# Two gate/up weight groups move from SP's DMA queue to ACT's, and score visits keep their order

## The chip, the cores and the metric

The kernel runs on one core of a Trainium2 chip. The metric is the device time of one execution in microseconds, lower is better. The core has a matrix engine (PE, with its weight loads as PEld), a vector engine (DVE), a scalar engine (ACT), GpSimd (POOL) and a queue engine (SP), which run their own instruction streams and wait for each other on semaphores. Transfers are done by 16 DMA engines; SP and ACT can both issue them.

## The reference, cut to what matters

```
x = A_x                                  # 1 x 2048 x 576, bf16
xn = layernorm(x)
q, k, v = split(xn @ wqkv)               # 32 heads of 18 columns
p = softmax(mask(q k^T / sqrt(18)))      # causal, a window of 256 positions
s = (p v) @ wo
h = sigmoid(xn @ w_gate) * (xn @ w_up)   # 2048 x 4608
g = silu(h @ w_down)
out = x + s * g
```

## The kernel before

The 2048 rows are worked in four chunks of 512 (`CH`, `NCH`), each of four blocks of 128 rows. A chunk goes through layer norm, the q, k and v projections, attention in 8 groups of four heads, the output projection (`wo`), the gate/up projection in 36 feature tiles of 128 (`build_ffn`), the down projection and the final product. The weights of gate and up come in 12 groups of three feature tiles into a ring of three slots (`RW`). `load9` brings one group (named `w:chunk:group`) with four DMAs of 240 or 192 KB, 884,736 bytes together.

The program first builds a list of operations with dependencies (`deps`, which become semaphore waits), order dependencies (`odeps`, which only tell the planner what comes first), an engine, a planned cost and a priority. `schedule()` then plans each engine's order with these costs, and `emit()` writes the engines' streams in that order. So a changed cost factor (`W_FACTOR` for weight loads, `XT_BYTES` for transposes) or a changed dependency can move work on all engines. DMA cost in the planner is one pipe in order of issue. In the kernel before every DMA is issued by SP.

What stands around the change, in the first chunk:

- `project` (L448) makes q, k or v of one block. q and k are copied (q by DVE at L490, k by ACT at L491) into `pk`, a ring of three slots (`RPK`), and a DMA transpose (L205, `qkt:chunk:block:q or k`) moves them into `qkp`, from which the scores read. The order of the projections is q0 q1 v0 v1 q2 v2 k0 v3 k1 q3 k2 k3 in the list (`QKV_FIRST`); a later one that takes the same `pk` slot waits for the transpose of the earlier one. k0 takes the slot of q0, k1 that of q1, q3 that of q2, k2 that of k0. v is copied by ACT (L513).
- `build_ffn` makes feature tile `ft` in steps `fa:c:ft`, `fb0:c:ft` and `fb1:c:ft` (L748), 18 matmuls per tile. The first step of a group's first tile (`fa:0:3` for the second group) waits for the group's four DMAs. ACT makes the tanh (L734), DVE the product (L738).
- `build_unit` makes one score visit (L556, `sc:c:heads:unit`; `pvsc` where it is merged with the value product of an earlier group, L639) into PSUM banks 0 to 3. ACT takes the exponentials (L579, two per visit), DVE the masks. The visits are filler between the gate/up steps, and the planner may take them in any order that their dependencies allow.
- The gate/up groups of the later chunks wait for a slot of the ring and for `w_gate`, a step of the down projection (L821).

Two places of the kernel before in its own words: after the second group's loads, the transposes from the third on are planned behind them,

```python
                    if c == 0 and fg == 1:
                        for o in self.op_qkt[QKT_BEHIND:]:
                            o.behind = ws[-1:]
```

and the banks that the down projection of a chunk's last block may take are

```python
            cands = ((0, 1), (2, 3)) if blocks[-1] == QPC - 1 else ((6, 7), (4, 5), (0, 1), (2, 3))
```

Of the kernel before, what the change touches and what calls it, by code (L numbers as in the profile page):

```python
# [15 lines left out]
QPC = CH // P  # L16
# [18 lines left out]
RW = 3  # L35
# [20 lines left out]
FB_CUTS = (0, 3, 7)  # L56
LAST = 448
W_GATE = 2

PRIO_NS = 40.0  # L60
SEM_NS = 50.0
DMA_SLACK_NS = 600.0
# [5 lines left out]
W_ISSUE_NS = 660.0  # L68
# [2 lines left out]
LATE_SLACK = 5000.0  # L71
LN_STEP = 1
XT_CUT = 4
QKT_BEHIND = 2
WARM = 10
X0_SLACK = 0.0
X_PRIO = (-9, -9, -9, -9)
QKV_LOAD = (-8, -4, -6)
W_PRIO = (-5, 2, 3)
WARM_NS = 427.0  # L80
W_FACTOR = 1.42
X0_FACTOR = 1.7
XT_BYTES = 1.2
DMA_LAT_NS = 1600.0
DMA_BYTES_PER_NS = 320.0

# [79 lines left out]
class Builder:  # L166
# [32 lines left out]
        return o  # L199

    def dma(self, dst, src, nbytes, name, lane, deps=(), prio=3, issue=DMA_ISSUE_NS, transpose=False,
            slack=DMA_SLACK_NS, eng="SP"):
        def fn(eng):
            if transpose:
                return eng.dma_start_transpose(dst, src)  # L205
            return eng.dma_start(dst, src)  # L206
        o = self.op(eng, issue, fn, name, deps, prio, nbytes=nbytes, lane=lane)
        o.slack = slack
        if lane not in self.lane_ids:
            self.lane_ids[lane] = len(self.lane_ids)  # L210
        return o
# [51 lines left out]
    def build(self):  # L263
        self.r_xr = Ring(NXR)
        self.r_xnr = Ring(NXNR)
        self.r_xn = Ring(1)
        self.r_w = Ring(RW)
        self.r_t = Ring(RT)
        self.r_pk = Ring(RPK)
        self.r_exp = Ring(NEXP)  # L270
        self.r_s = Ring(RS)
        self.r_xf = Ring(RXF)
        self.r_th = Ring(RTH)
        self.r_rec = Ring(RREC)
        self.r_bn = Ring(RBN)
        self.op_f1 = {}
        self.build_init()
        self.op_pv = [[None] * NHG for _ in range(NCH)]
        self.op_sc = [[[] for _ in range(NHG)] for _ in range(NCH)]
        self.op_on = [[None] * NHG for _ in range(NCH)]  # L280
        self.op_oc = [[[], []] for _ in range(NCH)]
        self.op_v = [None] * NQB
        self.op_tail = [None] * NHG
        self.op_hT = {}
        self.f2_last = None
        for c in range(NCH):
            self.build_ln(c)
            if c == 0:
                self.build_weights()
                self.build_wd()  # L290
            self.build_qkv(c)
            self.last_mul = None
            self.pending = None
            self.build_attn(c)
            if c == 0:
                self.op_wo = []
            self.build_wo(c)
            self.build_ffn(c)
            if c == 0:
                self.build_late_weights()  # L300
                for o in self.ops:
                    if o.name.startswith("wo:0:") and o.fence is None:
                        o.add_dep(self.op_wo)
# [27 lines left out]
            return r  # L331
        self.op_warm = self.pe(n * WARM_NS, f, name, deps=deps, prio=-9, psum=[ps])

    def load9(self, low, up, w_low, w_up, name, lane, deps, prio, factor=1.42):
        cols = w_low.shape[1]
        a = w_low.rearrange("(j p) c -> p j c", p=64)
        b = w_up.rearrange("(j p) c -> p j c", p=64)
        out = []
        for k, (dst, src, n) in enumerate(((low[:, 0:5, :], a[:, 0:NC:2, :], 5), (up[:, 0:4, :], b[:, 1:NC:2, :], 4),
                                           (low[:, 5:NC, :], a[:, 1:NC:2, :], 4), (up[:, 4:NC, :], b[:, 0:NC:2, :], 5))):  # L340
            out.append(self.dma(dst, src, factor * n * 64 * cols * 2, f"{name}.{k}", lane + (k,), deps=deps, prio=prio,
                                issue=W_ISSUE_NS))
        return out

    def build_weights(self):
# [137 lines left out]
    def build_qk(self, c, i, j, old):  # L483
        spk, dpk = self.r_pk.take()
        o, ps = self.project(c, i, j, f"qk:{c}:{i}:{j}", dpk, self.op_pv[c - 1][NHG - 1] if c > 0 else None)

        def f_ev(e):
            dst = self.pk[:, spk, :, 0:DH].rearrange("p (t h) d -> p t h d", t=2)
            if j == 0:
                return e.tensor_copy(dst, self.halves(ps))  # L490
            return e.activation(dst, self.halves(ps), ACTF.Copy)  # L491
        ev = self.rd("ACT" if j else "DVE", act_ns(D) if j else dve_ns(D), f_ev, f"qke:{c}:{i}:{j}",
                     deps=[o, self.op_pkz] + [t for t in (self.op_on[c - 1] if c > 0 else [])], prio=1, psum=[ps])
        c0 = j * CH + i * P
        dm = self.dma(self.qkp[:, :, c0:c0 + P], self.pk[:, spk, :, :].rearrange("p h d -> p (h d)"),
                      XT_BYTES * 8 * P * P * 2, f"qkt:{c}:{i}:{j}", ("qk", i, j), deps=[ev] + old, prio=0,
                      issue=XT_ISSUE_NS, transpose=True)
        self.r_pk.release(spk, dm)
        (self.op_q, self.op_k)[j].append(dm)
        self.op_qkt.append(dm)  # L500
        return o
# [40 lines left out]
    def build_unit(self, c, u, pieces, merge):  # L542
# [22 lines left out]
        if pend:  # L565
            self.pending = None
            o = self.pe(pend[1] + MODE_NS + nblk * P / 2.4 + 30, lambda e, a=pend[0], b=f_sc: (a(e), b(e))[1],
                        f"pvsc:{c}:{hgs[0]}:{u}", deps=pend[2] + deps, prio=0, psum=[pend[3], ps], mode=("c32", "r32"))
            pend[4](o)
        else:  # L570
            o = self.pe(nblk * P / 2.4 + 30, f_sc, f"sc:{c}:{hgs[0]}:{u}", deps=deps, prio=1, psum=[ps], mode="r32")
        for hg in hgs:
            self.op_sc[c][hg].append(o)
        exps = []
# [150 lines left out]
    def build_ffn(self, c):  # L725
# [25 lines left out]
        for ft in range(NFT + 1):  # L751
            if ft < NFT:
                if ft % FG == 0:
                    fg = ft // FG
                    sw, dw = self.r_w.take()
                    slots.append(sw)
                    wp = W_PRIO[fg] if c == 0 and fg < RW else -2
                    fc = slice(fg * FG * P, (fg + 1) * FG * P)
                    ws = self.load9(self.wgs[0:64, sw, :, :], self.wgs[64:P, sw, :, :], self.wg[:, fc],
                                    self.wu[:, fc], f"w:{c}:{fg}", ("w", sw),  # L760
                                    dw + ([self.w_gate] if c > 0 and fg < RW else []), wp)
                    dmas.append(ws)
                    if c == 0 and fg == 1:
                        for o in self.op_qkt[QKT_BEHIND:]:
                            o.behind = ws[-1:]
                pg.append(Psum((6,), (7,), (5,), (4,)))
                pu.append(Psum((6,), (7,), (5,), (4,)))
            war = [self.f2_last[ft // WDG]] if self.f2_last and ft < NFT else []

            def f_a(e, ft=ft):  # L770
                for i in range(NA):
                    if ft < NFT:
                        r = step(e, 0, ft, i)
                    if ft > 0:
                        r = step(e, 1, ft - 1, NC - NA + i)
                return r
            oa = self.pe(NA * mm_ns(CH), f_a, f"fa:{c}:{ft}",
                         deps=(dmas[ft // FG] + self.all_xn + war if ft < NFT else []), prio=3,
                         psum=[pg[ft]] if ft < NFT else [], mode="r64", odeps=mms)
            if ft > 0:  # L780
                pu[ft - 1].users.append(oa)
                if ft % FG == 0:
                    self.r_w.release(slots[ft // FG - 1], oa)
                th_mul(ft - 1, ob, oa)
            if ft == NFT:
                break

            def f_b(e, ft, i0, i1):
                for i in range(i0, i1):
                    step(e, 0, ft, NA + i)  # L790
                    r = step(e, 1, ft, i)
                return r
            ob = oa
            for n, (i0, i1) in enumerate(zip(FB_CUTS, FB_CUTS[1:])):
                ob = self.pe((i1 - i0) * mm_ns(CH), lambda e, ft=ft, i0=i0, i1=i1: f_b(e, ft, i0, i1), f"fb{n}:{c}:{ft}",
                             deps=[ob], prio=3, psum=[pu[ft]] if n == 0 else [], mode="r64")
                if n > 0:
                    pu[ft].users.append(ob)
            pg[ft].users.append(ob)
            self.op_f1[(c, ft)] = ob  # L800
            mms = [ob]
# [3 lines left out]
        self.f2_ops = f2_ops = {}  # L805
        prev = mms
        for blocks in (((0, 1), (2,), (3,)) if c == 0 else ((0,), (1,), (2,), (3,))):
            cands = ((0, 1), (2, 3)) if blocks[-1] == QPC - 1 else ((6, 7), (4, 5), (0, 1), (2, 3))
            banks = {i: Psum(*cands) for i in blocks}
            if c == NCH - 1 and blocks == (QPC - 1,):  # L810
                self.build_last(c, prev)
# [318 lines left out]
```

## Time and profile before

| what | value |
|---|---|
| median of 3 runs | 576.91 us (576.68 to 577.46) |
| profiled execution | 576.29 us |
| its span, first to last instruction | 574.5 us |
| mean granted PE clock | 0.998 |
| PE / ACT / DVE / POOL busy | 566.0 / 300.8 / 294.1 / 23.0 us |
| gate/up matmuls (L748) | 2592, 298.7 us busy |
| down projection matmuls (L821) | 1080, 135.0 us busy |
| q, k, v projection matmuls (L448) | 864, 55.3 us busy |
| score matmuls (L556) | 704, 36.1 us busy |
| bytes moved by DMA | 72.82 MB, mean 127 GB/s |

Matmuls overlap, so busy times of groups are sums of overlapped intervals. A wait of PE is idle time ahead of one of its instructions; the profile names what ended it where a semaphore event shows it, and writes "issue" where it shows none. The time of a DMA instruction on a queue is the time that its issue takes; "to landing" counts from the issue to the semaphore event of the data.

### The profile page before, as it was taken

The numbers are of one execution on the slowest core, as the hardware profiler recorded it, in microseconds if no ns is written. First come the engines' busy times: TensorE is split into PE (matmuls) and PEld (weight loads), VectorE is DVE, ScalarE is ACT, GpSimd is POOL, SyncE is SP. The second block draws the span as 40 slices with busy tenths as digits, with TensorE's granted clock in tenths as the row PEclk, the third lists the DMA queues.
The fourth block names the chain that finished last, engine by engine and source line by source line (L and its number), as shares of the span: only waits on it lengthen the run. The fifth ranks groups of instructions, "written<-read, shape, count | busy, mean of one in ns | idle before, by whom it ended". The sixth has DMA issues, their size and how long they took to land.

```text
span 574.5 us, 14808 instructions
## 1 busy us (share of the span) xinstructions
PE 566.0 (99%) x6350; PEld 274.7 (48%) x6350; DVE 294.1 (51%) x589; ACT 300.8 (52%) x403; POOL 23.0 (4%) x51
## 2 busy tenths in 40 slices
PE   8999999999999999999999999999999999999996
PEld 5544443457444444455753444344654444444554
DVE  5138877422247886621115888772122677774112
ACT  5357787214448887520307787760242778872201
POOL 3001110000001100000000011000000000000000
PEclk9999999999999999999999999999999999999999
DMA  8999999436935665341793666414479356651010
GB/s 203 200 214 251 224 211 232 88 63 119 198 80 135 146 156 126 79 87 42 140 206 91 146 138 151 106 50 100 56 135 186 84 124 138 134 126 40 1 42 21
DMA packets 124861, 72.82 MB, mean 127 GB/s; under 512 B 53630, under 2 KB 124286, under 8 KB 124798
## 3 DMA queue, kind: packets, MB, share of 16 engines
q1 hardware_dynamic: 124798, 71.90, 58.6%
q8 instruction: 50, 0.82, 0.6%
q14 instruction: 13, 0.11, 0.1%
HBM read 55.22 MB, written 2.36 MB: 100 GB/s over the span
## 4 chain that ended last, share of the span: by engine, by line
PE 95%; SPq 3%; DMA 1%; issue 0%; DVE 0%; ACT 0%
PE ps L748 50%; PE ps L821 23%; PE ps L448 8%; PE ps L556 5%; PE ps L639 4%; PE ps L705 3%; SPq L206 2%; PE ps L851 2%; DMA wgs<-in_B_w_up_dram 1%; SPq L205 1%; DVE thf L884 0%; ACT thf L882 0%; DVE thf L886 0%; DVE xf L888 0%
## 5 line engine op out<-in xcount | busy, mean ns | idle before, releaser
L748 PE MATMUL ps<-xn,wgs 64*128 64x512 bf16 x2592 | 298.7, 377 | 1.2 <-DMA wgs<-in_B_w_up_dram 1.2
L579 ACT ACTIVATE expr<-ps 128x1024 bf16<-128x1024 f32 (+1 forms) x184 | 174.9, 1003 | 45.3 <-PE ps L556 45.3
L748 PEld LDWEIGHTS ps<-xn,wgs 64*128 64x128 bf16 x2592 | 119.5, 94 | 152.3 <-issue 19.1
L821 PE MATMUL ps<-wd_sb,hT 128*128 128x512 bf16 (+1 forms) x1080 | 135.0, 287 | 0.0
L734 ACT ACTIVATE tring<-ps 128x512 bf16<-128x512 f32 x144 | 86.4, 600 | 62.6 <-PE ps L748 61.2
L611 DVE TENSOR_TENSOR expr<-expr,m 128x1024 bf16<-128x1024 bf16 (+1 forms) x152 | 81.9, 571 | 68.6 <-ACT expr L579 68.5
L738 DVE SCALAR_TENSOR_TENSOR hT<-tring,ps 128x512 bf16<-128x512 bf16 x144 | 97.0, 675 | 39.0 <-ACT tring L734 27.7
L821 PEld LDWEIGHTS ps<-wd_sb,hT 128*128 128x128 bf16 x1080 | 68.0, 98 | 66.3 <-issue 3.1
L882 ACT ACTIVATE thf<-ps 128x576 bf16<-128x576 f32 (+2 forms) x17 | 10.6, 622 | 110.6 <-PE ps L821 102.8
L884 DVE SCALAR_TENSOR_TENSOR thf<-thf,ps 128x576 bf16<-128x576 bf16 (+2 forms) x17 | 12.2, 719 | 90.0 <-ACT thf L882 89.9
L448 PE MATMUL ps<-wqkv_sb,xn 64*128 64x288 bf16 x864 | 55.3, 283 | 0.2 <-DMA wqkv_sb<-in_A_wqkv_dram 0.2
L448 PEld LDWEIGHTS ps<-wqkv_sb,xn 64*128 64x128 bf16 x864 | 42.9, 94 | 11.2 <-issue 1.3
L556 PE MATMUL ps<-qkp 18*128 18x384 bf16 (+2 forms) x704 | 36.1, 276 | 1.0 <-issue 1.0
L655 DVE STREAM_TRANSPOSE tf<-ps 128x512 f32<-128x512 f32 x32 | 22.9, 715 | 11.4 <-PE ps L556 9.9
L556 PEld LDWEIGHTS ps<-qkp 18*128 18x128 bf16 x704 | 10.8, 92 | 34.4 <-issue 20.8
L490 DVE CAST pk<-ps 128x576 bf16<-128x576 f32 x16 | 12.1, 756 | 28.8 <-PE ps L448 28.6
L639 PE MATMUL ps<-expr,vau 128*32 128x256 bf16 (+2 forms) x704 | 25.6, 277 | 0.0
L621 POOL COPY qkp<-qkp 128x256 bf16<-128x256 bf16 x24 | 11.5, 479 | 317.0 <-PE ps L556 317.0
L669 DVE STREAM_TRANSPOSE op__63<-pk 128x512 bf16<-128x512 bf16 x32 | 22.7, 708 | 1.1 <-DVE pk L663 0.2
L491 ACT ACTIVATE pk<-ps 128x576 bf16<-128x576 f32 x16 | 10.4, 652 | 22.6 <-PE ps L448 22.6
L639 PEld LDWEIGHTS ps<-expr,vau 128*32 128x32 bf16 x704 | 13.1, 97 | 15.3 <-ACT tring L734 6.8
L705 PE MATMUL ps<-wo_sb,oT 64*128 64x512 bf16 (+1 forms) x288 | 19.2, 283 | 0.0
(39 smaller groups left out, 142.6 us busy)
## 6 DMA issues: line engine op xcount, KB each, us to landing
wgs<-in_B_w_gate_dram SPq DMA_DIRECT2D x48, 240.0 KB, 3.8
wgs<-in_B_w_up_dram SPq DMA_DIRECT2D x48, 240.0 KB, 4.9
wgs<-in_B_w_up_dram SPq DMA_DIRECT2D x48, 192.0 KB, 4.0
wgs<-in_B_w_gate_dram SPq DMA_DIRECT2D x48, 192.0 KB, 4.5
wd_sb<-in_B_w_down_dram SPq DMA_DIRECT2D x9, 576.0 KB, 4.7
xf<-in_A_x_dram SPq DMA_DIRECT2D x18, 144.0 KB, 2.3
out_dram<-xf SPq DMA_DIRECT2D x15, 144.0 KB, 1.8
xr<-in_A_x_dram SPq DMA_DIRECT2D x14, 144.0 KB, 4.1
```

What stands on the lines that cost most here:

```text
L448: r = e.matmul(self.bank(ps, HV, hf), self.xn[r0:r0 + 64, k, i * P:(i + 1) * P], self.wqkv_sb[r0:r0 + 64, j, k, :], start=(k == 0), stop=( ...
L556: r = e.matmul(self.ps[:, b:b + n * P], self.qkp[r0:r0 + DH, hg, k0:k0 + P], self.qkp[r0:r0 + DH, hg, q0 * P:(q0 + n) * P], start=True, st ...
L579: return e.activation(self.expr[:, es, 2 * pr:2 * pr + 2, 0:nblk * P], src, ACTF.Exp, scale=SM_SCALE)
L611: return e.tensor_tensor(ap, ap, m, ALU.mult)
L639: r = e.matmul(self.ps[32 * j:32 * j + 32, b + q0 * P:b + (q0 + n) * P], vf[:, v0:v0 + 32], self.expr[:, es, j, pos * P:(pos + n) * P], st ...
L655: t1 = self.rd("DVE", dve_ns(CH), lambda e, ps=ps: e.transpose(tf.rearrange("p g d -> p (g d)"), self.bank(ps)), f"t1:{c}:{hg}", deps=[o_p ...
L669: t2 = self.op("DVE", dve_ns(CH), lambda e, on=on: e.transpose(self.op_[:, hg % NOT, :], on.rearrange("p g d -> p (g d)")), f"t2:{c}:{hg}" ...
L705: r = e.matmul(self.bank(ps2[w], n1 - n0, n), self.oT[r0:r0 + 64, kt, qi * P:(qi + 1) * P], self.wo_sb[r0:r0 + 64, kt, n0:n1], start=(swap ...
L734: return e.activation(self.tring[:, st_, :], self.bank(ps), ACTF.Tanh, scale=0.5)
L738: return e.scalar_tensor_tensor(self.hT[:, ft, :], self.tring[:, st_, :], 1.0, self.bank(ps), ALU.add, ALU.mult)
L748: return e.matmul(self.bank((pg, pu)[gu][ft]), self.wgs[r0:r0 + 64, slots[ft // FG], i, fl * P:(fl + 1) * P], self.xn[r0:r0 + 64, i, :], s ...
L821: r = e.matmul(self.ps[:, b + n0:b + n1], lhsT, self.wd_sb[:, q, fl, n0:n1], start=(ft == 0), stop=(ft == NFT - 1))
```

## The change

- The four DMAs of the second and the third group of the first chunk (`w:0:1`, `w:0:2`) are issued by ACT, with an order dependency: the second group after ACT's copy of v's first block, the third after ACT's copy of k's first block. No wait comes with it.
- The transposes are no longer planned behind the second group (`QKT_BEHIND` 99).
- Each score visit gets an order dependency on the visit built before it.
- The planner's cost of weight loads and transposes rises a little, and the down projection of a chunk's last block may take banks 4 to 7 too.

The built order that results, in the first chunk, on ACT: copy of v0, DMA, copy of v1, DMA, copy of v2, DMA, copy of v3, DMA, tanh of tile 0, copy of k0, DMA, copy of k1, tanh of tile 1, DMA, DMA, DMA, tanh of tile 2. On SP: six transposes in a row (q0, q1, q2, k0, k1, q3) after the last load of wqkv, then the fourth gate/up group, then the transposes of k2 and k3. On PE (matmul counts; gu is L748, qkv L448, sc L556, pv L639, f2 L821):

```
before: qkv126 (with 4 blocks' transposes) gu26 qkv36 gu36 qkv18 gu36 qkv36 gu8  sc4 gu28 sc8 gu26 sc8 gu22 sc8 gu32 pv16 ...
after:  qkv126 (with 4 blocks' transposes) gu26 qkv36 gu12 qkv18 gu36 qkv36 gu86 sc8 gu22 sc8 gu24 sc8 gu26 sc4 gu18 pv16 ...
```

The qkv18 is q3, the last qkv36 is k2 and k3. The first step of the second group is reached after 52 gu matmuls. The last value product of the first chunk, between 28 and 28 gu matmuls before, stands after 8 f2 matmuls in the changed kernel; the third chunk's output projection, after the next chunk's projections before, stands ahead of the down projection.

```diff
+W_ACT = {1: lambda b: [b.op_v[0]], 2: lambda b: [b.op_ev[(0,0,1)]]}
...
-QKT_BEHIND = 2
+QKT_BEHIND = 99
...
-W_FACTOR = 1.42
+W_FACTOR = 1.46
...
-XT_BYTES = 1.2
+XT_BYTES = 1.25
...
     def dma(self, dst, src, nbytes, name, lane, deps=(), prio=3, issue=DMA_ISSUE_NS, transpose=False,
-            slack=DMA_SLACK_NS, eng="SP"):
+            slack=DMA_SLACK_NS, eng="SP", odeps=()):
...
-        o = self.op(eng, issue, fn, name, deps, prio, nbytes=nbytes, lane=lane)
+        o = self.op(eng, issue, fn, name, deps, prio, nbytes=nbytes, lane=lane, odeps=odeps)
...
-    def load9(self, low, up, w_low, w_up, name, lane, deps, prio, factor=1.42):
+    def load9(self, low, up, w_low, w_up, name, lane, deps, prio, factor=1.46, eng="SP", odeps=()):
...
-                                issue=W_ISSUE_NS))
+                                issue=W_ISSUE_NS, eng=eng, odeps=odeps))
...
                       issue=XT_ISSUE_NS, transpose=True)
+        self.op_ev[(c, i, j)] = ev
         self.r_pk.release(spk, dm)
...
             o = self.pe(nblk * P / 2.4 + 30, f_sc, f"sc:{c}:{hgs[0]}:{u}", deps=deps, prio=1, psum=[ps], mode="r32")
+        if self.visit:
+            o.odeps.append(self.visit)
+        self.visit = o
...
-                                    dw + ([self.w_gate] if c > 0 and fg < RW else []), wp)
+                                    dw + ([self.w_gate] if c > 0 and fg < RW else []), wp,
+                                    **(dict(eng="ACT", odeps=W_ACT[fg](self)) if c == 0 and fg in W_ACT else {}))
...
-            cands = ((0, 1), (2, 3)) if blocks[-1] == QPC - 1 else ((6, 7), (4, 5), (0, 1), (2, 3))
+            cands = ((0, 1), (2, 3), (6, 7), (4, 5)) if blocks[-1] == QPC - 1 else ((6, 7), (4, 5), (0, 1), (2, 3))
```

More of the change, by code (lines that the diff above doesn't have):

```diff
@@ L276, in build @@
         self.op_f1 = {}
+        self.op_ev = {}
+        self.visit = None
         self.build_init()
```

## The prediction

> **What bounds the kernel now.** I read the page first: engines, then the chain that ended last.
>
> ```profile
> PE 566.0 (99%) x6350; PEld 274.7 (48%) x6350; DVE 294.1 (51%) x589; ACT 300.8 (52%) x403; POOL 23.0 (4%) x51
> ...
> PE 95%; SPq 3%; DMA 1%; issue 0%; DVE 0%; ACT 0%
> ```
>
> TensorE (PE) is busy for 566.0 of 574.5 us and is 95% of the chain. The built order of the changed kernel has the same 6,350 matmuls of the same shapes and, like the kernel before, 255 places where the kind of matmul changes. So no matmul time is saved; the change can only remove waits of PE, or add some. The waits of PE (waiter, releaser, total, times, longest) are few:
>
> ```profile
> PE ps L748 <- DMA wgs<-in_B_w_up_dram: 1.2, 1, 1.2
> PE ps L556 <- issue: 1.0, 1, 1.0
> PE ps L448 <- DMA wqkv_sb<-in_A_wqkv_dram: 0.2, 1, 0.2
> ```
>
> Both large ones lie in the first 40 us, so next I read the timeline there (start, duration, engine and line; the idle time before is in brackets):
>
> ```profile
> 14.12 3.97 SPq L205 DMA_TRANSPOSE qkp<-pk  x2
> 18.14 0.60 SPq L206 DMA_DIRECT2D wgs<-in_B_w_gate_dram  x1
> ...
> 20.11 0.62 SPq L206 DMA_DIRECT2D wgs<-in_B_w_up_dram  x1
> 20.77 1.34 SPq L205 DMA_TRANSPOSE qkp<-pk  x1
> ...
> 19.43 0.29 PE L448 MATMUL ps<-wqkv_sb,xn 64*128 64x288 bf16 x1
> ...
> 26.02 1.26 PE L748 MATMUL ps<-xn,wgs 64*128 64x512 bf16 x10 [1.19 <-DMA wgs<-in_B_w_up_dram]
> ...
> 39.70 0.40 PE L556 MATMUL ps<-qkp 18*128 18x256 bf16 x8 [0.97 <-issue]
> ```
>
> The second gate/up group (w:0:1) can be issued only at 18.14, after two transposes; its last load, issued at 20.11, lands 5.6 us later and PE stands for 1.19 us. At 39.70 the score visit of 8 matmuls x 256 columns is the planner's sc:0:0:2, placed ahead of its elders; it needs the transpose of k2, issued at 34.71, which took 4.9 us and landed at 39.61. That is the 0.97 us without a named releaser. A third one, k2's projection at 31.95, waited 0.18 us for a transpose that frees its pk slot. From there to the end PE shows no wait.
>
> Last, the DMA engines in stretches (stretch, length, busy us and count of each engine, TensorE clock, DMA share, GB/s):
>
> ```profile
> 17.50:18.00 0.50, 0.50 (x8) 0.26 (x6) 0.00 (x0) 0.00 (x0) 0.00 (x0) 1.00 0.31 30
> 24.50:25.00 0.50, 0.34 (x3) 0.00 (x0) 0.00 (x0) 0.12 (x1) 0.00 (x0) 1.00 0.20 20
> 25.00:25.50 0.50, 0.00 (x0) 0.00 (x0) 0.00 (x0) 0.48 (x1) 0.00 (x0) 1.00 0.07 18
> 8.00:16.00 8.00, 7.81 (x126) 6.23 (x125) 2.95 (x6) 4.55 (x9) 0.55 (x1) 1.00 1.13 233
> ```
>
> From 8 to 16 us they move 233 GB/s and are full. [...]
>
> **The change, part by part.**
>
> *Group w:0:1 to ACT.* Its four issues leave SP (18.14 to 20.73) and stand on ACT behind each of the four v evictions, which begin at 13.54, 14.64, 15.74 and 16.85, last 0.65 us and have 0.45 us of idle time between them. With 0.62 us per issue (the SP rows; ACT issues none before) each pair takes 1.27 us against a spacing of 1.10, so the evictions slip by 0.17, 0.34 and 0.51 us. What waits for them has room: v1's banks go to the first gate/up step at 16.64 (eviction over at 15.46), v2's to the second near 18.3 (16.7), v3's to k1's projection near 20.7 (18.0). Cost nothing; without this cover up to 0.5 us. The last load is issued near 17.5 to 18.1 instead of 20.11. With the 5.6 us that it took it lands by 23.7, before PE asks for it. PE asks later, too: q3's projection (18 matmuls, 1.10 us to the next start at 27.10) now stands ahead of the group's first step, so 24.84 becomes 25.9. The wait of 1.19 us goes, with over 2 us to spare.
>
> *Group w:0:2 to ACT.* One issue behind k0's eviction, three behind the second tanh: 3 x 0.62 = 1.9 us of ACT. The next tanh is due only after q3 and 14 gate/up matmuls, about 3 us on. Nothing. The group landed by 31.1 before and is first needed after four more gate/up blocks; nothing there either.
>
> *Transposes alone on SP.* Six follow each other; SP waits only for the evictions. q2's, issued at 20.77 before, can go at 18.1. So k2's wait of 0.18 us should go.
>
> *Score visits chained.* The first visit now stands behind 86 gate/up matmuls instead of 8: from k2 and k3 on that is 86 x 0.108 = 9.3 us (the spacing of starts: 1.94 us for 18), and all eight transposes were done 6.5 us after k3's projection even with loads between them (34.3 to 40.8). The 0.97 us goes, 1.04 with the start-to-start excess (1,345 ns against 308 elsewhere).
>
> *What the new order moves later.* The last value product of the first chunk falls among the down-projection's matmuls; the third chunk's output projection moves ahead of them, 106 gate/up matmuls behind the last value product where the second and fourth chunk had 110 and no wait. At the starts of the later chunks two visits stand closer (20 gate/up matmuls; or 8 down and 8 gate/up), with a final tanh (0.65 us) in ACT's order beside them. A visit's exponentials end 2.4 us after its start (151.65 to 154.04); the closest new spacing is about 2.5 to 2.7 us. So 0 to 0.3 us at each of three starts; I take 0.2 in all, bounds 0 and 1.0.
>
> *The exposed edge: k0's projection.* It reuses the pk slot of q0 and so waits for q0's transpose. That one was issued at 14.12 and took 5.2 us (landed 19.29); PE was there at 19.43. 0.14 us of room is all. Now loads from a second queue run beside it, and no row shows two queues of bulk loads. Rows of transposes to landing: 3.1 us with nothing beside (128.21), 5.2 here, 6.0 with a load group around it (20.77), 9.2 behind a long run of loads (153.06). Below: 3.1 gains nothing, PE is not there sooner. Above: 9.2 lands at 23.3, 3.9 us late; the same comes from 884,736 bytes of w:0:1 at 220 GB/s, 4.0 us, all going first. I take the 6.0 row, since it too shares its time with one group: 20.09, a wait of 0.66 us. For a better case speak the stretches at 30 to 18 GB/s, which a second queue can fill.
>
> [...]
>
> **Sum.** 1.19 + 1.04 + 0.18 = 2.41 us gone, 0.66 + 0.2 new: 1.55 us less. The profiled execution took 576.29 us (span 574.5, 1.8 around it), so 574.74; the median 576.91 lies 0.62 above it: 575.4.
>
> **Rivals.**
>
> *Full contention: k0 waits for q0's transpose (slower).* From about 15 us the loads of w:0:1 share the engines with wqkv's k part and the transposes; if both queues get equal turns, nearly all 4.0 us of the group pass before q0's transpose is done, at 23.3, and k0 is 3.9 us late. Net 3.9 + 0.2 - 2.41 = +1.7: 578.6. It decides from a landing at 21.6 on (19.43 + 2.2). For it: full engines from 8 to 16 us, and 0.14 us of room. And the one packet of another queue that runs among loads (queue q8, 16 KB at 22.70) takes 1.35 us (5.3% of 16 engines over 1.6 us) against 0.88 where hardly anything else moves (128.37; 5.0% over 1.1 us), and the group that it met ended late: engine time is shared, not added. Against it: the near-idle stretch from 17.5 to 18.0, which the second queue could use.
> [...]
>
> *Half of it.* Transpose at 21 to 22, k0 1.5 to 3 us late: between -0.7 and +0.8, 576.2 to 577.7, no change that can be told.
>
> [...]
>
> **Chances.** Forecast, k0 at most 1 us late: 0.48. Half contention or blocked issues: 0.20. Full contention: 0.32. About 0.2% (1.15 us) is what a measurement of this kernel can tell from no change; so faster 0.48, same 0.20, slower 0.32. The forecast's own range is 574.3 (no cost at all, 2.41 gone) to 575.8; the whole range reaches to full contention, 578.7.
>
> **What would show it.** Right: no wait at the first step of w:0:1, its last load landing before 24, q0's transpose landing by 20.5, no unnamed wait at the first score visits. Wrong: idle time ahead of L448 near 19.4 with a transpose as releaser, or v evictions more than 0.6 us apart from v's matmuls, or PE waits at the starts of the later chunks above 0.3 us each.

## The result and the profile after

The changed kernel takes 582.11 us (median of 6 executions, 581.2 to 582.93) against 577.23 for the kernel before on the same chip (6, 576.68 to 578.07): ratio 1.0084, 95% interval 1.0071 to 1.0098. It is 0.8% slower, and the prediction was 575.4 with a range to 578.7. The profiled execution took 581.56 us, span 579.6, 5.1 more than before.

The page first: PE's busy time, its clock in 40 slices, and the chain.

```profile
PE 566.1 (98%) x6323; PEld 275.5 (48%) x6350; DVE 297.4 (51%) x589; ACT 298.4 (51%) x403; POOL 21.9 (4%) x51
...
PEclk9799999999999999999999999999999999999999
...
PE 95%; SPq 2%; DMA 2%; issue 1%; DVE 0%; ACT 0%
```

PE seems as busy as before (566.1 against 566.0 us), but 27 matmul records are missing, all of the down projection (L829: 131.9 us busy against 135.0), and the projections' time rose (L451: 57.1 against 55.3). So part of the loss is waited and part is slower work. The second slice of the clock, 14.5 to 29 us, shows 7 tenths. The waits of PE (waiter, releaser, total, times, longest):

```profile
PE ps L451 <- DMA qkp<-pk: 4.2, 1, 4.2
PE ps L829 <- issue: 1.6, 10, 0.2
PE ps L755 <- DMA wgs<-in_B_w_up_dram: 0.4, 1, 0.4
```

One wait counts (L829's are ten gaps of at most 0.2 us, in the line whose records are missing). L451 is the projection, L755 gate/up, L560 the scores in this kernel's numbering. The waits at w:0:1, at k2 and at the early visit are gone. The timeline around the new one (start, duration, engine and line, idle time before it):

```profile
13.39 20.34 SPq L206 DMA_TRANSPOSE qkp<-pk  x6
...
13.51 0.71 ACTq L207 DMA_DIRECT2D wgs<-in_B_w_gate_dram  x1
14.60 0.65 ACT L517 ACTIVATE vau<-ps 128x576 bf16<-128x576 f32 x1 [0.45 <-PE ps L451]
...
16.82 0.60 ACTq L207 DMA_DIRECT2D wgs<-in_B_w_up_dram  x1
...
17.20 3.18 PE L755 MATMUL ps<-xn,wgs 64*128 64x512 bf16 x26 [0.43 <-DMA wgs<-in_B_w_up_dram]
24.57 4.50 PE L451 MATMUL ps<-wqkv_sb,xn 64*128 64x288 bf16 x36 [4.19 <-DMA qkp<-pk]
28.84 1.73 PE L755 MATMUL ps<-xn,wgs 64*128 64x512 bf16 x12
```

k0 stands 4.19 us for q0's transpose, and then k0 and k1 (36 matmuls) take 4.27 us from their start to the next line. The chain has the releaser, and the windows (stretch, length, busy us and count of PE, PEld, DVE, ACT, POOL, then PE's clock, DMA share, GB/s) the clock:

```profile
13.39 11.05 DMA qkp<-pk
...
24.57 4.50 PE ps L451 x36
```

```profile
20.00:22.00 2.00, 0.38 (x2) 0.00 (x0) 0.66 (x1) 0.00 (x0) 0.00 (x0) 1.00 1.15 211
22.00:24.00 2.00, 0.00 (x0) 0.00 (x0) 0.00 (x0) 0.00 (x0) 0.00 (x0) 0.63 1.23 194
24.00:26.00 2.00, 1.43 (x14) 1.04 (x16) 0.00 (x0) 0.00 (x0) 0.00 (x0) 0.50 1.25 211
26.00:28.00 2.00, 2.00 (x20) 1.45 (x18) 0.00 (x0) 0.65 (x1) 0.00 (x0) 0.50 0.32 69
28.00:30.00 2.00, 2.00 (x20) 1.15 (x18) 0.00 (x0) 0.65 (x1) 0.00 (x0) 0.66 0.92 168
```

q0's transpose took 11.05 us (5.2 before) and landed at 24.43. While PE idled, its granted clock fell to 0.5, from 22.54 to 29.37 by the clock records. Last, which queue's packets moved (q1 is SP's, q10 ACT's; packets, MB, share of 16 engines), first from 13.5 to 18.5 us, then from 18.5 to 21, then from 21 to 24:

```profile
q1 hardware_dynamic: 1859, 0.88, 127.3%
q8 instruction: 1, 0.02, 1.7%
```

```profile
q10 hardware_dynamic: 342, 0.26, 71.5%
q1 hardware_dynamic: 512, 0.13, 38.3%
```

```profile
q10 hardware_dynamic: 830, 0.60, 109.5%
q1 hardware_dynamic: 50, 0.01, 11.3%
```

ACT issued from 13.51 on, yet none of its packets moved before 18.5. Then both queues moved packets, and from 21 to 24 us ACT's loads had the engines nearly alone: 830 packets against 50 of SP's queue, which held the transposes. By 24 us 1172 of the group's 1216 packets had moved, though q0's transpose was issued first and still had not landed. w:0:1's loads landed at 22.2 to 25.33.

**The account**, by the starts of the second chunk's projections (130.88 against 125.97, +4.91): first gate/up matmul 0.56 later (w:0:0's last load at 16.95 instead of 16.17); k0 delayed by its wait, 4.37 from start to start; k0 and k1 4.27 instead of 2.21 us (the latter from the kernel of e14 below), +2.06; 0.2 at the next gate/up matmuls. Less the three waits removed, 2.41: +4.8. From there to the end +0.1.

### The profile page after: what moved, and what is told of

Same layout as the page of the kernel before. It is cut to its first block, busy times and chain, and to the rows that moved or that the text cites. A ratio compares the mean times of both kernels' runs of the same rounds, so it can differ in the third digit from the quotient of the medians.

```text
span 579.6 us, 14791 instructions
## 1 busy us (share of the span) xinstructions
PE 566.1 (98%) x6323; PEld 275.5 (48%) x6350; DVE 297.4 (51%) x589; ACT 298.4 (51%) x403; POOL 21.9 (4%) x51
## 4 chain that ended last, share of the span: by engine, by line
PE 95%; SPq 2%; DMA 2%; issue 1%; DVE 0%; ACT 0%
PE ps L755 50%; PE ps L829 23%; PE ps L451 8%; PE ps L560 5%; PE ps L646 4%; PE ps L712 3%; SPq L207 2%; DMA qkp<-pk 2%; PE ps L859 2%; DVE thf L892 0%; ACT thf L890 0%; DVE thf L894 0%; DVE xf L896 0%
## 5 line engine op out<-in xcount | busy, mean ns | idle before, releaser
L755 PE MATMUL ps<-xn,wgs 64*128 64x512 bf16 x2592 | 298.5, 377 | 0.4 <-DMA wgs<-in_B_w_up_dram 0.4
L755 PEld LDWEIGHTS ps<-xn,wgs 64*128 64x128 bf16 x2592 | 119.3, 94 | 152.2 <-issue 20.9
L829 PE MATMUL ps<-wd_sb,hT 128*128 128x64 bf16 (+1 forms) x1053 | 131.9, 284 | 2.5 <-issue 1.6
L829 PEld LDWEIGHTS ps<-wd_sb,hT 128*128 128x128 bf16 x1080 | 67.9, 98 | 66.2 <-issue 3.1
L451 PE MATMUL ps<-wqkv_sb,xn 64*128 64x288 bf16 x864 | 57.1, 289 | 4.3 <-DMA qkp<-pk 4.2
L451 PEld LDWEIGHTS ps<-wqkv_sb,xn 64*128 64x128 bf16 x864 | 43.2, 96 | 17.2 <-issue 6.1
L560 PE MATMUL ps<-qkp 18*128 18x384 bf16 (+2 forms) x704 | 36.1, 275 | 0.0
L560 PEld LDWEIGHTS ps<-qkp 18*128 18x128 bf16 x704 | 10.7, 92 | 33.3 <-issue 19.3
```

The lines of the kernel that those rows point to most:

```text
L451: r = e.matmul(self.bank(ps, HV, hf), self.xn[r0:r0 + 64, k, i * P:(i + 1) * P], self.wqkv_sb[r0:r0 + 64, j, k, :], start=(k == 0), stop=( ...
L560: r = e.matmul(self.ps[:, b:b + n * P], self.qkp[r0:r0 + DH, hg, k0:k0 + P], self.qkp[r0:r0 + DH, hg, q0 * P:(q0 + n) * P], start=True, st ...
L755: return e.matmul(self.bank((pg, pu)[gu][ft]), self.wgs[r0:r0 + 64, slots[ft // FG], i, fl * P:(fl + 1) * P], self.xn[r0:r0 + 64, i, :], s ...
L829: r = e.matmul(self.ps[:, b + n0:b + n1], lhsT, self.wd_sb[:, q, fl, n0:n1], start=(ft == 0), stop=(ft == NFT - 1))
```

## The experiments

Three theories were put to the test. **1:** w:0:1, issued by ACT, delays q0's transpose on SP, and that is where the time goes (not the chaining or the new order). **2:** about 2 us of it is the clock, halved because PE idled. **3:** ACT's loads are held while SP issues transposes. Ratios are to the kernel before on the same chip, with the 95% interval. Line numbers differ a little from kernel to kernel. An order made by hand moves an operation in an engine's planned list and leaves the rest.

### Taking the loads off ACT

**e1: w:0:1 back on SP, all else as after.**

```diff
+    put([f"w:0:1.{k}" for k in range(4)], "ACT", "SP", "qkt:0:1:0")
...
     b.schedule()
+    move(b)
```

> Kernel after with one thing moved: the four loads of w:0:1 are taken out of ACT's stream and put into SP's, right behind the transpose of q1 (where the kernel before has them); every other order, the chained score visits and w:0:2 on ACT included, is that of after. Theory 1 (the 4.19 us that k0 waits in after come from w:0:1 in ACT's queue passing q0's transpose, and they bring the halved clock with them): q0's transpose lands about 5.2 us after its issue as in before (11.05 in after), k0 waits under 0.3 us, the granted clock stays at 1.0 over 22 to 30 us, the first step of w:0:1 waits about 1.2 us again, and the time is 575.5 to 577 us. Rival (the loss comes from the chained visits, from w:0:2 on ACT or from the new order of the other transposes): k0 still waits 3 us or more, or it doesn't and the time is still above 580.

Measured 582.71 us, 1.0097 (1.0081 to 1.0113). The first half of theory 1 came as expected: q0's transpose landed 6.5 us after its issue and k0 had no wait for it. The time did not come, since w:0:2, still on ACT, was now issued at 21.54, next to q2's transpose, and the wait moved one projection on:

```profile
22.43 1.46 PE L755 MATMUL ps<-xn,wgs 64*128 64x512 bf16 x11
31.29 2.34 PE L451 MATMUL ps<-wqkv_sb,xn 64*128 64x288 bf16 x18 [7.40 <-DMA qkp<-pk]
```

7.40 us at q3, and q3's 18 matmuls took 2.34 us against 1.28 in before, at a granted clock of 0.50 (30 to 34 us). The same collision, with another group and another transpose.

**e2: only the last two loads of w:0:1 on SP.** Same edit with `.2` and `.3`.

> Kernel after with only the last two loads of w:0:1 moved to SP's stream behind q1's transpose; the first two stay on ACT, at 13.5 and 14.6 us. Theory 1 with a price by bytes (what the transpose waits for is the loads ahead of it in the other queue): q0's transpose lands about 2 us earlier than in after (22 to 23 us), k0 waits 2 to 2.5 us, and the time is 578 to 580 us. Rival (any load that waits in ACT's queue costs the transpose the whole delay): lands at 24 us or later, k0 waits 4 us, 581 to 582.5. Whether 2 us of idle TensorE is enough to halve the granted clock is open: after lost it behind 4.19 us of idle time, before kept it behind 1.19.

578.54 us, 1.0032 (1.002 to 1.0045): in the range of theory 1, but not by its price. In the profiled execution (580.49, the longest of six) the transpose still landed at 23.72 and k0 waited 3.58 us. So bytes alone did not set the delay: with half of them the landing came 0.7 us earlier.

**e7: no load on ACT, everything else planned as in after.**

```diff
-W_ACT = {1: lambda b: [b.op_v[0]], 2: lambda b: [b.op_ev[(0,0,1)]]}
+W_ACT = {}
```

> Kernel after with no load issued by ACT (w:0:1 and w:0:2 on SP's queue behind the three q transposes); chained visits and the changed planning factors stay. Theory 1: transposes as quick as in before (q0's lands 5 to 5.5 us after its issue), no wait of k0, clock at 1.0; w:0:1 lands about 1.5 us later than in before, so its first step waits some 2.5 us; with the chaining's own price of 1.7 us in the kernel before chained, 577.5 to 580 us. Rival (the chaining or the new order makes the loss of after): 581 to 583.

576.68 us, 0.9998 (0.9989 to 1.0007): level with before and, by the two ratios, 5.0 us below after. This is the whole loss, taken away by one line (the planner then puts both groups on SP behind the three q transposes); the rest of the change costs and brings nothing together. q0's transpose landed 6.2 us after its issue and k0 had no wait. What is left in the profiled execution (579.24, the longest of 11) is a wait for w:0:1:

```profile
PE ps L755 <- DMA wgs<-in_B_w_up_dram: 2.6, 1, 2.6
```

The forecast was too dark, since it added the 1.7 us that chaining costs in e4.

**e4: before with the chaining alone** (the three lines with `self.visit`).

> Kernel before with only the chaining of the score visits added; all loads and transposes stay on SP as in before. Theory 1 and the prediction's sum: the early wait of the third score visit (1.04 us) is gone and nothing else changes at the start, starts of later chunks cost up to 0.2 us, so 576.0 to 576.7 us against 577.2 for before. Rival (chaining is itself part of the loss): 577.5 or more.

578.9 us, 1.0025 (1.0013 to 1.0036), a miss: chaining costs here. The first visit in order now waits itself for the last transposes, and w:0:1's wait was 1.81 us in this execution:

```profile
26.77 1.25 PE L752 MATMUL ps<-xn,wgs 64*128 64x512 bf16 x10 [1.81 <-DMA wgs<-in_B_w_up_dram]
...
41.84 0.40 PE L557 MATMUL ps<-qkp 18*128 18x384 bf16 x8 [0.79 <-DMA qkp<-pk]
```

By the ratio the cost is 1.4 us, by the medians 1.7. Against before the second chunk starts 0.6 us late, and another 1.1 us come by the end, 0.7 of them in the last chunk, whose output projection this order breaks up.

**e12: after without the chaining; e15: e7 without the chaining.**

> Kernel after without the chaining of the score visits (the planner then starts with sc:0:1:4 four steps earlier); ACT's loads stay. Theory 1: the collision at q0's transpose and the halved clock are untouched (k0 waits 4 us, clock 0.5 for 6.8 us), and the first visits now wait as well, so 582 to 584 us. Rival (the chaining makes the loss, as the 1.7 us of the kernel before chained could suggest): 580 or less.

583.55 us, 1.011 (1.0096 to 1.0123), k0's wait 4.66 us: theory 1, the collision does not need the chaining.

> The kernel with no load issued by ACT (576.68 us, level with before), and without the chaining of the score visits, so that only the planning factors and the three q transposes ahead of w:0:1 are left of the change. It tells what the chaining is worth where no load goes by ACT. The prediction's step (chaining takes away a wait of 1.04 us of a visit that comes too early): about 1.0 us slower than 576.7. Rival (the chaining costs more than it brings, as before chained at +1.4 us suggests): 575.5 or less.

578.65 us, 1.0031 (1.0017 to 1.0045). With this order chaining is worth 1.9 us by the ratios, nearly twice the step's figure, though not by the early visit (no visit waits in e15): its profile shows four later waits, 1.2 us together. What chaining does depends on the order that the planner makes of it.

### Taking k0's dependence away

**e5: own buffers.** k0, k1 and q3 of the first chunk are copied into memory that is unused then, so no early projection waits for a transpose. All queues and orders as in after.

```diff
+        x = self.oT[:, 0:4, :].rearrange("p (s a) (h d) -> p s (a h) d", s=2, d=HP)
+        y = self.op_[:, 0:2, :].rearrange("p a (h d) -> p (a h) d", d=HP)[:, None, :, :]
+        self.pkx = {(0, 0, 1): (x, 0), (0, 1, 1): (x, 1), (0, 3, 0): (y, 0)}
...
+        buf, at = self.pkx.get((c, i, j), (self.pk, spk))
```

> Kernel after, with the projections k0, k1 and q3 of the first chunk copied into memory that is still unused then (parts of oT and op_, zeroed by two added memsets on POOL at the start), so that none of the first projections waits for a transpose to free a pk slot; the order of every engine and queue is that of after, and w:0:1 still goes by ACT's queue. Theory 1 (what delays q0's transpose is w:0:1 in the other queue, and what it costs is k0's wait for the slot, with the clock halved behind that wait): q0's transpose still lands at 22 us or later, yet k0 starts without a wait, the granted clock stays at 1.0, and the time falls by 4.2 + 2.2 us from 582.1 to about 575.7 (575 to 577). Rival (the late transposes themselves set the time through the first score visits, or the loss lies elsewhere in the new order): the wait reappears at the first score visit and the time stays above 579.

577.48 us, 1.0024 (1.0005 to 1.0043), spread over 576.17 to 581.47: just outside the expected 575 to 577. The added memsets on POOL held up the first xn, and gate/up began at 18.61 instead of 16.64. The profiled execution (576.17) shows no wait of PE for any transfer:

```profile
PE ps L835 <- issue: 1.6, 10, 0.2
PE ps L338 <- DVE neghalf L310: 1.5, 1, 1.5
PE ps L435 <- DVE xnr L412: 0.7, 1, 0.7
```

Its last matmuls come 0.3 us earlier than before's despite the start 2.0 us late: 2.3 us gained in this execution, the fastest of 12, close to the predicted sum of 2.41. The transposes fared better in it, too (q0's landed 6.6 us after its issue), so it does not show what the buffers do against a late transpose; e9 does.

**e9: the same, zeroed by ACT, so that the start is not delayed.**

> As the kernel with own buffers (after, with k0, k1 and q3 of the first chunk copied into unused parts of oT and op_), but the two added memsets are done by ACT behind its own first memset, where it idles until 6.4 us, instead of by POOL, which had delayed the first xn and moved the first gate/up matmul from 16.6 to 18.6 us. Theory 1 and the prediction's sum: start as in before, and the sum of the three waits of before (1.19 + 1.04 + 0.18) is gained in full, 574.5 to 575 us in runs where no other wait appears. Rival (ACT's loads beside SP's transposes still make q3's, k2's or the first visits' transposes late in part of the executions): a spread of 574.5 to 579 and a median of 576 to 577.

583.5 us, 1.01 (1.0083 to 1.0116): both expectations missed. q0's transpose landed at 24.59, and nothing waited for it; but PE came early to the first visit, and there

```profile
45.41 0.40 PE L566 MATMUL ps<-qkp 18*128 18x384 bf16 x8 [4.65 <-DMA qkp<-pk]
```

the transposes, beside both groups on ACT, were awaited after all (in e10, with no load on ACT, the first visit starts at 42.28), and the 24 gate/up matmuls behind the visit took 4.45 us against 2.76 in e10. The buffers did not remove the collision; they moved the wait to the next reader.

### The clock

**e3: after with 32 matmuls, whose result nobody reads, ahead of k0.**

> Kernel after with 32 matmuls added on TensorE that write a PSUM bank nobody reads, right ahead of k0, so that TensorE works (about 3.85 us at 120 ns each) instead of idling until q0's transpose lands. No load or transpose moves. Theory 2 (about 2.2 us of the loss are the halved clock behind the 4.19 us of idle time: k0 and k1 took 4.28 us for 36 matmuls against 2.2): the granted clock stays near 1.0 from 22 to 30 us, k0 and k1 take about 2.2 us, and the time is about 579.9 us (579.3 to 580.6). Rival (the 4.28 us have another cause, such as operands or DMA traffic): k0 and k1 still take over 4 us and the time is 582 us or, if the added matmuls overrun the wait, more.

582.45 us, 1.0091 (1.0064 to 1.0118): undecided by the time. The 32 matmuls took 4.09 us, and k0 ran at a granted clock of 1.00 (24 to 26 us), but q1's transpose landed later than in after, and the idle time and the halved clock (0.50 from 28 to 30 us) came at k1:

```profile
24.49 1.28 PE L451 MATMUL ps<-wqkv_sb,xn 64*128 64x288 bf16 x18 [0.53 <-DMA qkp<-pk]
28.14 2.34 PE L451 MATMUL ps<-wqkv_sb,xn 64*128 64x288 bf16 x18 [2.37 <-DMA qkp<-pk]
```

The same 18 matmuls: 1.28 us behind work, 2.34 behind idleness.

**e13 and e14: before, with 4.2 us ahead of k0, once idle, once busy.** No transfer changes.

In e13 k0 waits for three chained memsets on POOL; in e14 35 matmuls into an unread PSUM bank stand ahead of it.

```diff
+    for k, n in enumerate((4, 4, 1)):
+        o = Op("POOL", 0, lambda e, n=n: e.memset(b.oT[:, 0:n, :], 0.0), f"hold{k}", [last], 0)
...
+    t["qk:0:0:1"].deps = t["qk:0:0:1"].deps + [last]
```

```diff
+        for k in range(35):
+            r = e.matmul(b.ps[:, 1536:1536 + HV], b.xn[:, k % 4, 0:P], b.wqkv_sb[:, 0, k % 4, :], start=True, stop=True)
```

> Kernel before with k0 made to wait, without any change to a load or transpose: three memsets on POOL, chained, start when the first gate/up matmuls that stand ahead of k0 are done (about 1.8 + 1.8 + 0.5 us, so some 4.2 us in which TensorE has nothing to do), and k0 waits for them. 4.2 us of delay here take the place of the 1.19, 1.04 and 0.18 us of waits that follow it in before, so 1.8 us are left of it. Theory 2 (idle time of this length at this place halves the granted clock for 3.4 or 6.8 us and costs up to 2.2 us more): clock 0.5 behind it as in after, and 577.2 + 1.8 + 1 to 2.2, so 580 to 581.2 us. Rival (the halved clock of after has to do with its transfers, not with idleness): clock at 1.0, 579.0.

> The pair of the run before it: kernel before with the same 4.2 us put ahead of k0 as work, 35 matmuls of 120 ns that write a PSUM bank nobody reads. Theory 2: the clock stays at 1.0 and 1.8 us are left, so 579.0 us (578.5 to 579.5), 1 to 2.2 us less than with the same time idle. Rival: the two agree within 0.5 us.

e13 581.51 us, 1.0071 (1.0056 to 1.0087), a little above theory 2's range; e14 578.92, 1.0032 (1.0022 to 1.0042), within it. The first two lines are of e13's timeline, the others of e14's:

```profile
24.55 3.97 PE L448 MATMUL ps<-wqkv_sb,xn 64*128 64x288 bf16 x36 [4.46 <-POOL oT L1100]
28.35 4.06 PE L748 MATMUL ps<-xn,wgs 64*128 64x512 bf16 x36
```

```profile
19.83 4.46 PE L1099 MATMUL ps<-wqkv_sb,xn 128*128 128x288 bf16 x35
24.23 2.38 PE L448 MATMUL ps<-wqkv_sb,xn 64*128 64x288 bf16 x36
26.44 4.05 PE L748 MATMUL ps<-xn,wgs 64*128 64x512 bf16 x36
```

Two things are shown. Busy, the 4.4 us (19.83 to 24.23) cost 1.96: the later waits (2.41) take up the rest, as the sum said. Idle, the same delay costs 2.6 us more by the medians and 2.0 in the profiled executions (580.77 against 578.74). Of the 2.0, 0.3 is a longer wait and 1.6 the halved clock: k0 and k1 take 3.80 us from their start to the next line instead of 2.21, at a granted clock of 0.61 from 24 to 26 us and 0.54 from 26 to 28 (1.00 in e14). Four of e13's six executions had a lower mean clock than the profiled one (0.994 against 0.996). Theory 2 holds, with every load and transpose on SP as in before. In after the mean clock was 0.991 to 0.994 in all executions (before: 0.998 in its profile, and 0.997 to 1.0 in all but one of its executions beside the experiments), so it is there each time.

### The two queues

**e8: w:0:1 on ACT up front** (its four loads behind the third copy of xn in ACT's list).

> Kernel after with the four loads of w:0:1 still issued by ACT but up front, right behind its third copy of xn (near 10 us), while SP issues only plain loads. Theory 3 (ACT's loads were held for 5 us in after, from their issue at 13.5 until 18.5, because SP's transposes were being issued and held up the descriptors behind them): ACT's first packets appear within 1.5 us of their issue and share the engines with SP's loads; w:0:0 and wqkv1 land later by up to the 5.5 us that w:0:1's 1.2 MB take at 215 GB/s, and the time is 577 to 582. Rival (ACT's queue waits for what SP's queue has been given before, whatever it is): ACT's first packets still appear near 18 us.

581.79 us (578.46 to 585.08, 4 executions), 1.0066 (1.0042 to 1.0089). The loads were issued at 8.25 to 10.37, and their first packet came at 10.55, 2.3 us after the first issue (1.5 had been expected by theory 3) instead of 5.1. From 11 to 18 us the packets of the two queues, both plain loads:

```profile
q10 hardware_dynamic: 1054, 0.77, 59.0%
q1 hardware_dynamic: 1015, 0.73, 53.9%
```

Nearly equal here, loads beside loads. Loads beside transposes differ from profile to profile: where after moved 830 packets of ACT's loads and 50 of SP's queue from 21 to 24 us, e12 in the same stretch moved

```profile
q1 hardware_dynamic: 780, 0.19, 62.7%
q10 hardware_dynamic: 421, 0.30, 62.5%
```

and q0's transpose took as long there, 11.0 us.

For theory 3 speak the first packets of after (5.1 us behind the issue) and e5 (3.6), against 2.3 here. Against it speak the profiles of e12, e3 and e9, where SP issued the same transposes and the first packets came 2.6, 2.9 and 2.8 us behind the issue (at 16.06, 16.48 and 16.62). There q0's transpose landed at 24.35, 24.35 and 24.59 all the same. So theory 3 is not shown, and the transpose is as late without a late first packet.

The time was no better: q0's transpose now stood behind all the loads (landed at 24.08), and the first gate/up step waited 1.87 us for w:0:0, in the profiled execution, the longest of the four. And w:0:2, still on ACT, met a later transpose: k3 waited 2.95 us for one that took 9.4, and its 18 matmuls took 2.34 us against 1.28 for k2 ahead of it. (The expectation counts 1.2 MB for w:0:1; its four loads are 0.88 MB, 4.1 us at 215 GB/s.)

### Where the predicted gain goes

These kernels have no load on ACT, and try to take the waits of before.

**e6: before, own buffers, q3 moved up into w:0:1's wait.**

> Kernel before, all loads and transposes on SP's queue as there, no chaining, with the same three projections copied into unused memory and the projection q3 moved up to ahead of the first step that needs w:0:1. Theory 1 and the prediction's reading of before (1.19 us of waiting for w:0:1's last load and 0.18 for a slot): q3's 1.1 us of matmuls lie in that wait, so 576.0 to 576.3 us against 577.2. Rival (the wait moves on: to the step behind q3, since the load lands no earlier and what follows was already waiting for w:0:2 or the transposes): 577 or more.

577.23 us, 1.0011 (1.0001 to 1.002): the rival. w:0:1's wait fell to 0.31 us, and the early visit's grew:

```profile
26.62 5.14 PE L754 MATMUL ps<-xn,wgs 64*128 64x512 bf16 x46 [0.31 <-DMA wgs<-in_B_w_up_dram]
...
40.26 0.40 PE L562 MATMUL ps<-qkp 18*128 18x256 bf16 x8 [1.99 <-issue]
```

**e10 and e11: e7 with own buffers and k2, k3 moved up; in e10 w:0:1 between the transposes of q1 and q2.**

> No load issued by ACT, chained visits, own buffers zeroed by ACT, w:0:1 on SP between the transposes of q1 and q2 as in before, and the projections k2 and k3 moved up in TensorE's order to ahead of the first step that needs w:0:1 (2.2 us of matmuls in place of the wait for w:0:1's last load). Theory: transposes as quick as in before, w:0:1's last load landed by 25.7 to 26.5 us with q3, k2 and k3 (3.3 us) done before its first step, no early score wait: 1.19 + 1.04 + 0.18 gained, 574.5 to 575.2 us, with little spread. Rival (the wait moves on to w:0:2 or to the first visit): 576 or more.

> As the run before it in this list, but with w:0:1 behind all three q transposes, as the changed planner puts it: it lands some 1.5 to 2.5 us later (28.7 us in the kernel with no load issued by ACT, whose first step waited 2.6 us). With k2 and k3 (2.2 us) ahead of that step, theory: the wait shrinks from 2.6 to about 0.4 us and the time is 574.3 + 0.4, about 575 us; rival (the wait moves on to w:0:2): 576 or more.

577.55 us, 1.0012 (1.0 to 1.0024), and 578.02, 1.0016 (1.0005 to 1.0026): the rivals. No wait for w:0:1 in either; the first visit waits instead, as in e10:

```profile
42.28 0.40 PE L566 MATMUL ps<-qkp 18*128 18x384 bf16 x8 [2.89 <-DMA qkp<-pk]
```

**e16: e10 with three visits moved by hand behind w:0:3's first step. e17, e18: e10 with the first visit told to come behind step 9, and the planner spacing the others.**

```diff
+    t["sc:0:0:0"].odeps.append(t["fb0:0:9"])
```

That is e17; e18 has `fb1:0:9` there.

> The kernel with no load issued by ACT, own buffers and k2, k3 moved up (577.55 us, whose first score visit waited 2.89 us for k3's transpose, landed at 42.1), with the first three visits and their exponentials and masks put some 1.5 steps later, behind the first matmuls that need w:0:3. Theory (all transfers of the start run at some 200 GB/s through 42 us, so time gained ahead of that point comes back as a wait for whichever transfer is last; only work that needs none of the late transfers can fill it): w:0:3's last load lands at 40.6 and its first step waits under 1 us, the visits no longer wait, so about 2 us less, 575.3 to 576 us. Rival (the wait moves on once more, to w:0:4 or to the visits' exponentials): 577 or more.

578.48 us, 1.0021 (1.0011 to 1.0031). The visit's wait for the transpose fell to 0.27 us, but the visits lay too close, and two of them waited 2.6 us for exponentials.

> As the kernel with no load issued by ACT, own buffers and k2, k3 moved up (577.55 us), but the planner is told that the first score visit comes behind the second matmul group of step 9, and so spaces all visits of the first chunk some one step (1.95 us of TensorE) later by itself, with their exponentials; the hand-moved visits of the run before waited 2.6 us for their exponentials, which lay too close. Theory (the first visit waits for the last transfer of the start, k3's transpose at 41.5 to 42.1 us): w:0:3's step waits under 1 us, the visit under 0.5, the exponentials not, so 577.55 - 2.9 + 0.8 = 575.4 us (575 to 576), below both kernels. Rival (later visits give the time back at the end of the chunk): 577 or more.

> The same with the first visit one matmul group later (behind all of step 9; 0.55 us more of TensorE's work ahead of it). Theory: the visit no longer waits in any execution, and the time agrees with the run before it within 0.5 us. Rival: later by as much as the visits are moved, 0.5 us or more slower than the run before it.

576.66 us, 0.9996 (0.9983 to 1.001), and 576.48, 0.9995 (0.9976 to 1.0014). The best here, single executions at 575.3 to 575.6, but level with before by the interval, and above e17's expected 575 to 576. The start went as planned, and e17's profile shows the time coming back 50 us later, at another weight group:

```profile
40.53 1.25 PE L761 MATMUL ps<-xn,wgs 64*128 64x512 bf16 x10 [0.24 <-DMA wgs<-in_B_w_up_dram]
42.00 0.40 PE L566 MATMUL ps<-qkp 18*128 18x384 bf16 x8 [0.22 <-DMA qkp<-pk]
...
92.62 1.25 PE L761 MATMUL ps<-xn,wgs 64*128 64x512 bf16 x10 [1.61 <-DMA wgs<-in_B_w_up_dram]
```

No version was found that beats both kernels by more than its interval.

## Why the prediction was wrong, point by point

- **The step that failed** is "I take the 6.0 row, since it too shares its time with one group: 20.09, a wait of 0.66 us". It measured 4.19 us (4.37 from start to start), with the landing at 24.43. The row was of one queue, where that transpose stood behind one group's loads and was done 6 us after its issue. With a second queue, loads issued after the transpose passed it, and it took 11.05 us (10.3 to 11.2 in e2, e3, e9 and e12 too). Even the upper bound, 23.3, was 1.1 us short: it priced the group's 4.0 us of engine time and no more. Where the 1.1 us come from is open; ACT's late start at 18.5 is not needed for them, since e12, e3 and e9 started at 16.1 to 16.6 and landed no earlier.
- **A term was missing.** No part of the sum, and no rival, priced what idleness does to the clock: 2.06 us at k0 and k1 in after, 1.6 in the profiled executions of e13 against e14. Rival "Full contention" had the wait and +1.7; with the wait as it was, the clock, and w:0:0's 0.56 it comes to the +4.8 of the account.
- "The stretches at 30 to 18 GB/s, which a second queue can fill": wrong. The stretch is there again (21 GB/s from 18.0 to 18.5), with four loads waiting in ACT's queue.
- *Group w:0:1 to ACT.* The evictions slipped by nothing (13.50, 14.60, 15.71, 16.81): each issue, 0.60 to 0.77 us, ran beside the eviction ahead of it instead of behind it. So the blocked issues, which share the 0.20 of the chances, did not come either. The last load landed at 25.33, not "by 23.7"; its wait went because PE was later still.
- *Group w:0:2 to ACT*, "nothing there": true of after only because k0's wait had put its issue off to 26.96 to 31.62. In e1 it cost 7.40 us of waiting.
- *The three waits removed:* gone in after; and worth 2.41 together, as e14 (4.4 us of delay cost 1.96) shows and e5's fastest execution (2.3 us gained) agrees with. But e6, e10 and e17 show that a gain taken there mostly returns as a wait for a later transfer. The sum treated them as three separate costs; they are one supply that runs just behind.
- *Chained visits:* the early wait went in after, and chaining alone cost 1.4 us in before (e4) and saved 1.9 in e15's order. 1.04 was right for no order that was run without the collision.
- *Later chunks,* 0.2: 0.1 measured.
- *The range:* with no cost at all the sum's own terms give 576.91 - 2.41 = 574.5, not 574.3. It changes nothing here.
- *Equal turns of the two queues,* the "if" of the rival "Full contention" that puts the landing at 23.3: no run shows them between transposes and loads. There the counts go both ways (50 to 830 and, before that, 512 to 342 in after; 780 to 421 in e12), and the landing came 1.1 us later than the rival had it. Loads beside loads were near equal in e8 (1054 to 1015 packets). And nothing was won by the second queue: e7, without it, is 5.0 us below after and level with before.

## What to carry to other kernels

Do not start bulk loads from a second queue while transfers that the busiest engine waits for are under way in the first: here such a transfer took 11.05 us beside them instead of 5.2 to 6.5 without, and the wait of 4.19 us cost another 2.06 by the clock. When a wait is to be removed, ask which transfer is needed next and when it lands; with the transfers just in time, the wait only changes its place. And where a change leaves PE idle, ask what the clock may add behind it (half clock behind 2.37 us in e3 and 4.46 in e13, none behind 2.89 in e10), or put work there.

## What the runs showed of the hardware

- **PE's granted clock fell to half behind some waits of PE and not behind others.** In after it was 0.5 from 22.54 to 29.37 us, with PE idle from 20.38 to 24.57; in e13 it was 0.61 from 24 to 26 us and 0.54 from 26 to 28 behind 4.46 us of idle time; in e1 0.50 from 30 to 34 behind 7.40; in e3 0.50 from 28 to 30 behind 2.37. In the profiled executions of e10 and e15, which waited 2.89 and 2.39 us, the mean clock was 1.0; in before it was 1.00 behind the wait of 1.19 (26 to 30 us). So the length of the wait alone does not tell; what decides is not shown.
- **q0's transpose took about twice as long in four kernels whose loads, issued after it, ran on the other queue:** 11.0 to 11.2 us in after, e3, e9 and e12, against 5.2 in before and 6.2 to 6.5 in e1, e7 and e10. Loads beside loads moved nearly equal counts in e8 (1054 to 1015 packets); loads beside transposes moved 830 to 50 in after and 421 to 780 in e12, and what decides it stays open. e2, where half the group gave 10.3 us, and e5, where all of it gave 6.6, say that it is not bytes alone.
- **In after an issue on ACT ran beside the ACT instruction ahead of it:** 0.71 us of issue at 13.51 beside an eviction at 13.50 that took its usual 0.65. It was over before the next eviction could start (14.22 against 14.60), so whether it would hold that up is not shown.
